# First MoE: layer norm results copied by DMA into float32r tiles, whose transposes use that type

## The chip, the cores and the metric

The kernel runs on one core of one Trainium2 chip. The metric is the device time of one execution in microseconds (us). The engines are named as in the profile: PE is TensorE (PEld its weight loads), DVE VectorE, ACT ScalarE, POOL GpSimd, SP SyncE, which here only issues DMAs.

## What is computed

Attention with a bias from positions (4 batches, 8 heads, 576 positions, head size 64) gives x of 2304 tokens by 512. Two feed-forward layers follow. The first (d_ff 1024) is the one that the change touches, the second has d_ff 2048.

```python
def _moe_ref(x, w_in, w_out, g_ln):
    h = x @ w_in
    h_max = np.max(h, axis=-1, keepdims=True)
    e = np.exp(h - h_max)
    sm = e / (np.sum(e, axis=-1, keepdims=True) + 1e-09)
    solu = h * sm
    mu = np.mean(solu, axis=-1, keepdims=True)
    var = np.mean((solu - mu) ** 2, axis=-1, keepdims=True)
    ln = (solu - mu) / np.sqrt(var + 1e-06) * g_ln
    return (ln @ w_out).astype(np.float32)

def _moe2_ref(x, w_in, w_out):
    h = x @ w_in
    g = np.where(h >= 1, h, np.where(h <= -1, 0.0, (h + 1) ** 2 / 4))
    return (g @ w_out).astype(np.float32)
```

## The kernel before

Most products run in float32r, a float32 of reduced precision: each operand is split into a high part that fits the type and the rest, and a product is three products (high by high, high by rest, rest by high). `g_ln` is multiplied into `w_out` when that is split.

The first MoE works on 18 tiles of 128 tokens, i = 0 to 17. All engines' instructions stand in the order in which the code issues them (the order is written out by hand), and each engine runs its own queue in that order. The functions, by their steps:

- `split_x(i)` splits x of tile i: ACT L528, POOL L529.
- `emit_h(i)` makes h: 24 products of 512 columns on PE (L545) into the PSUM tile `ps_s` (two buffers).
- `emit_post(i)` is softmax, product and layer norm in five steps: DVE L563 (maximum) and ACT L564 (exp); DVE L566, L567, L568 (h times softmax, into the SBUF tile `sc` of 128×1024 float32); DVE L572 and ACT L573 (squares); DVE L575 and POOL L578 (the root); ACT L580 and L581, which write the normalised tile over `sc`. Tiles 0 and 1 use the attention's buffers (`e`), the others the pool `wb`, in which `sc` has three buffers.
- `emit_lt(i)` transposes the tile: eight transposes of 128×128 on PE (L687) into two PSUM tiles `ps_t`, then for each ACT L691 (high part, float32r) and DVE L695 (rest).
- `emit_o(p, half)` multiplies two tiles by `w_out`: 48 products of 256 columns on PE (L706) into `ps_x`, of which there is one buffer; ACT L711 copies it to SBUF and a DMA on ACT's queue (L712) writes it to DRAM.
- `split_w` (`bw`) prepares the second MoE's weights beside all that, by pieces: DVE L302, L305 and L306, ACT L310, DVE L312, POOL L315, ACT L321, POOL L292, with loads and stores on SP's queue.

The loop L752 runs over i = 2 to 17. In iteration i stand h of i, the first step of `emit_post(i)`, the last step of `emit_post(i - 1)` (L580, L581: `drain(bl)`), the transposes of tile i − 2, the middle steps of `emit_post(i)`, the output of a pair (from i = 4 on), and between them three to four steps of `split_w`, four more after every odd i. Behind the loop come the transposes of tiles 16 and 17 and the last four outputs.

DMAs issued by SP and ACT take eight semaphores in turn, so an issue also waits until the transfer that last used its semaphore has landed.

Of the kernel before, what the change touches and what calls it, by code (L numbers as in the profile page):

```python
# [11 lines left out]
F32 = mybir.dt.float32  # L12
F32R = mybir.dt.float32r
# [22 lines left out]
def tile_attention_moe_moe(  # L36
# [11 lines left out]
    nc = tc.nc  # L48
# [3 lines left out]
    def pool(name, side="left", space=None):  # L52
        if space == bass.MemoryType.DRAM:
            return tc.tile_pool(name=name, bufs=1, space=space)
        if space is not None:
            return tc.tile_pool(name=name, bufs=1, space=space, reuse_waits="tile")
        return tc.tile_pool(name=name, bufs=1, side=side, reuse_waits="tile")

    def opened(p):
        es = ExitStack()  # L60
        return es, es.enter_context(p)
# [4 lines left out]
    def flat(ap):  # L66
        return ap.rearrange("p a b -> p (a b)")

    def step(g, n=1):
        for _ in range(n):  # L70
            next(g, None)

    def drain(g):
        for _ in g:
            pass
# [7 lines left out]
    ident = const.tile([128, 128], F32, name="ident")  # L83
# [43 lines left out]
    for _ in range(8):  # L127
# [8 lines left out]
        out=dg[:, 0:32], in_=ident.rearrange("p (a h) -> p h a", a=4), axis=AX.X, op=ALU.max  # L136
# [7 lines left out]
    for _ in range(12):  # L144
# [8 lines left out]
        out=w2b,  # L153
# [227 lines left out]
    def ps_t():  # L381
        return ps.tile([128, 512], F32, tag="t", name="ps_t", bufs=3)
# [38 lines left out]
    def emit_exp(k):  # L421
        u, n = divmod(k, 9)
        i, h0 = divmod(n, 2)
        e, su = e_t[u, i][:, h0, :], su_t[u]
        nc.scalar.activation(  # L425
            out=e, in_=e, func=ACTF.Exp, scale=-1.0, bias=su[:, n:n + 1], accum_out=su[:, 9 + n:10 + n]
        )
# [85 lines left out]
    def split_x(i):  # L513
        if i < 2:
            xh = wq.tile([128, S + 64 * i], F32R, tag=f"kh{i}", name="xh", bufs=2)[:, 0:512]
            xl = wq.tile([128, S + 64 * i], F32R, tag=f"kl{i}", name="xl", bufs=2)[:, 0:512]
            xh = xh.rearrange("p (k t) -> p k t", k=KD)
            xl = xl.rearrange("p (k t) -> p k t", k=KD)
        else:
            xh = wb.tile([128, KD, 128], F32R, tag="xh", name="xh", bufs=2)  # L520
            xl = wb.tile([128, KD, 128], F32R, tag="xl", name="xl", bufs=2)
        t0 = 128 * i
        while t0 < 128 * i + 128:
            b, s0 = divmod(t0, S)
            n = min(S - s0, 128 * i + 128 - t0)
            o = t0 - 128 * i
            src = xb_t[b][:, :, s0:s0 + n]
            nc.scalar.copy(out=xh[:, :, o:o + n], in_=src)  # L528
            nc.gpsimd.tensor_tensor(  # L529
                out=xl[:, :, o:o + n], in0=src, in1=xh[:, :, o:o + n].bitcast(F32), op=ALU.subtract  # L530
            )
            t0 += n
        xs_t[i] = (xh, xl)
# [3 lines left out]
    def emit_h(i):  # L537
        xh, xl = xs_t.pop(i)
        h = ps_s()
        hp_t[i] = h  # L540
        for hf in range(2):
            c0 = hf * 512
            for kk in range(KD):
                for j, (l, r) in enumerate(((xh, wih), (xh, wil), (xl, wih))):
                    nc.tensor.matmul(  # L545
                        h[:, hf, :], lhsT=l[:, kk, :], rhs=r[:, kk, c0:c0 + 512],
                        start=kk == 0 and j == 0, stop=kk == KD - 1 and j == 2,
                    )
            yield

    def emit_post(i):
        h = hp_t.pop(i)
        if i < 2:
            e, sc = [
                flat(wa.tile([128, 2, S], F32, tag="e", name="e", bufs=EB))[:, 0:F1].rearrange("p (a c) -> p a c", a=2)
                for _ in range(2)
            ]
            st = wa.tile([128, 32], F32, tag="su", name="st", bufs=3)
        else:
            e = wb.tile([128, 2, 512], F32, tag="e", name="eb", bufs=1)  # L560
            sc = wb.tile([128, 2, 512], F32, tag="sc", name="scb", bufs=3)
            st = wb.tile([128, 8], F32, tag="st", name="stb", bufs=4)
        nc.vector.tensor_reduce(out=st[:, 0:1], in_=h, axis=AX.XY, op=ALU.max, negate=True)  # L563
        nc.scalar.activation(out=e, in_=h, func=ACTF.Exp, bias=st[:, 0:1], accum_out=st[:, 1:2])  # L564
        yield
        nc.vector.tensor_scalar(out=st[:, 2:3], in0=st[:, 1:2], scalar1=1e-9, scalar2=None, op0=ALU.add)  # L566
        nc.vector.reciprocal(out=st[:, 2:3], in_=st[:, 2:3])  # L567
        nc.vector.tensor_tensor_reduce(  # L568
            out=sc, in0=h, in1=e, scale=st[:, 2:3], scalar=0.0, op0=ALU.mult, op1=ALU.add, accum_out=st[:, 3:4]
        )  # L570
        yield
        nc.vector.tensor_scalar(out=st[:, 4:5], in0=st[:, 3:4], scalar1=-1.0 / F1, scalar2=None, op0=ALU.mult)  # L572
        nc.scalar.activation(out=e, in_=sc, func=ACTF.Square, bias=st[:, 4:5], accum_out=st[:, 5:6])  # L573
        yield
        nc.vector.tensor_scalar(  # L575
            out=st[:, 5:6], in0=st[:, 5:6], scalar1=1.0 / F1, scalar2=1e-6, op0=ALU.mult, op1=ALU.add
        )
        nc.gpsimd.tensor_tensor(out=st[:, 6:7], in0=st[:, 5:6], in1=mhalf, op=ALU.pow)  # L578
        yield
        nc.scalar.activation(out=st[:, 7:8], in_=st[:, 4:5], func=ACTF.Identity, scale=st[:, 6:7])  # L580
        nc.scalar.activation(out=sc, in_=sc, func=ACTF.Identity, scale=st[:, 6:7], bias=st[:, 7:8])  # L581
        ln_t[i] = sc
        yield

    EB, LT, LP = 4, 5, 7
    NK = NU * 9
    load_v(1)
    h_t, ln_t, lt_t, x2_t = {}, {}, {}, {}
# [7 lines left out]
    for k in range(NK + LP + 1):  # L596
        u, n = divmod(k, 9)
        hp, b = divmod(u, B)
        if k == NK:
            emit_T(k - LT)  # L600
            drain(bw)
            drain(emit_h(0))
            bp = emit_post(0)
        for c in order[n] if k < NK else tail.get(n, "TP"):
            if c == "Q":
                emit_qk(k)
                if b == B - 1 and hp + 1 < HP:
                    load_bias(hp + 1, n)
            elif c == "T" and 0 <= k - LT < NK and k != NK:
                emit_T(k - LT)  # L610
            elif c == "E":
                emit_exp(k)
            elif c == "P" and 0 <= k - LP < NK:
                u2, n2 = divmod(k - LP, 9)
                if n2 in (3, 7, 8):
                    emit_pv(u2, n2 // 4)
            elif c in "rRMSN" and u > 0:
                emit_norm(u - 1, c)
            elif c == "B":
                step(bg)  # L620
            elif c == "W" and k >= 6:
                step(bw)
        if k in (NK - 8, NK - 6):
            split_x(0 if k == NK - 8 else 1)
        if k > NK:
            step(bp)
        if k == NK + LT - 1:
            drain(emit_h(1))
            drain(bp)
            es_q.close()  # L630
            es_b, wb = opened(pool("wb"))
            split_x(2)
            bp = emit_post(1)
        elif k == NK + LT + 1:
            split_x(3)
        if n == 5 and 1 <= u < NU - 1:
            load_v(u + 1)
# [35 lines left out]
    def emit_lt(i):  # L673
        ln = flat(ln_t.pop(i))
        p, o = divmod(i, 2)
        if o == 0:
            lt_t[p] = (
                wb.tile([128, K1, 256], F32R, tag="lh", name="lh", bufs=2),
                wb.tile([128, K1, 256], F32R, tag="ll", name="ll", bufs=2),
            )  # L680
        lh, ll = lt_t[p]
        subs = []
        for q in range(2):
            tp = ps_t()
            for j in range(4):
                f = 4 * q + j
                nc.tensor.transpose(tp[:, j * 128:(j + 1) * 128], ln[:, f * 128:(f + 1) * 128], ident)  # L687
            t3 = tp.rearrange("p (f t) -> p f t", f=4)
            dh = lh[:, 4 * q:4 * q + 4, 128 * o:128 * o + 128]
            dl = ll[:, 4 * q:4 * q + 4, 128 * o:128 * o + 128]  # L690
            nc.scalar.copy(out=dh, in_=t3)  # L691
            subs.append((dl, t3, dh))
        yield
        for dl, t3, dh in subs:
            nc.vector.tensor_tensor(out=dl, in0=t3, in1=dh.bitcast(F32), op=ALU.subtract)  # L695
# [56 lines left out]
    for i in range(2, NTT):  # L752
# [6 lines left out]
        if i + 2 < NTT:  # L759
            split_x(i + 2)  # L760
        bp = emit_post(i)
        lt = emit_lt(i - 2)
        step(bp)
# [106 lines left out]
    for s in range(len(seq) + L2):  # L870
        if s < len(seq):
            j, f = seq[s]
# [83 lines left out]
```

## Time and profile before

| what | us |
|---|---|
| median of 3 runs | 977.04 (975.93 to 978.26) |
| profiled execution: its time | 977.47 |
| profiled execution: its span | 975.7 |
| PE busy | 942.9, 97% |
| ACT busy | 545.9, 56% |
| DVE busy | 616.0, 63% |
| POOL busy | 299.9, 31% |

A profile is one execution. Times in its rows count from the start of the span. The time of the execution is 1.8 us longer than the span. A matmul's end is modelled and matmuls overlap in the array, so the distance between two starts tells what one costs, not its duration. ACTq marks what ACT's sequencer does, here the issue of a DMA. In brackets behind a row stands the idle time of the engine before it and what ended that.

### The profile page before, as it was taken

What the parts mean: (1) busy time and instruction counts of PE and PEld (TensorE: products, weight loads), DVE (VectorE), ACT (ScalarE), POOL (GpSimd) and SP (SyncE); (2) the same over time, 40 slices, a digit from 0 to 9 for tenths busy, and PEclk for the clock granted to TensorE, in tenths of its full rate; (3) what the DMA queues carried; (4) which work ended last, traced back from release to release, by engine and by line L of the source; (5) the groups of instructions that cost most, each with busy time, mean ns of one, the idle gap of its engine ahead of it and who ended that gap; (6) DMA issues with size and microseconds to landing.
All of it is one profiled execution on the core that took longest, in us unless ns stands there. A gap on an engine that the chain in (4) does not pass through costs nothing.

```text
span 975.7 us, 15942 instructions
## 1 busy us (share of the span) xinstructions
PE 942.9 (97%) x5972; PEld 780.6 (80%) x5972; DVE 616.0 (63%) x1285; ACT 545.9 (56%) x1132; POOL 299.9 (31%) x255
## 2 busy tenths in 40 slices
PE   7779999999999999999999999899999999999998
PEld 5228888888788878999898988678888888888897
DVE  7988779779789536777776747774434343434343
ACT  5888888889889847666666533343222232222232
POOL 1015555555555213455565523430010011000000
PEclk9999999999999999999999999999999999999999
DMA  4895463563652100244554578501000100100010
GB/s 129 249 291 190 136 217 138 167 211 103 196 190 90 37 22 1 87 131 151 174 172 153 168 290 296 174 1 65 11 12 1 65 22 0 44 16 6 1 44 23
DMA packets 48034, 109.11 MB, mean 112 GB/s; under 512 B 7314, under 2 KB 12434, under 8 KB 47956
## 3 DMA queue, kind: packets, MB, share of 16 engines
q1 hardware_dynamic: 42688, 101.72, 32.0%
q10 hardware_dynamic: 4900, 4.72, 1.4%
q0 software_dynamic: 368, 1.64, 0.5%
q8 instruction: 47, 0.77, 0.3%
q14 instruction: 31, 0.25, 0.1%
HBM read 77.25 MB, written 30.82 MB: 111 GB/s over the span
## 4 chain that ended last, share of the span: by engine, by line
PE 74%; DVE 11%; issue 5%; POOL 4%; ACT 4%; DMA 2%; SPq 0%; POOLq 0%; DVEq 0%; ACTq 0%
PE acc L855 17%; PE h L831 17%; PE ps_s L545 8%; PE ps_s L404 7%; PE ps_x L496 6%; PE ps_x L706 5%; PE ps_t L467 5%; POOL wp L315 2%; DVE r L255 2%; PE ps_x L500 2%; DVE raw L305 2%; PE ps_t L443 1%; PE o L268 1%; POOL wdl L292 1%; DVE wp L302 1%
## 5 line engine op out<-in xcount | busy, mean ns | idle before, releaser
L838 DVE SCALAR_TENSOR_TENSOR ga<-ga 128x512 f32<-128x512 f32 (+1 forms) x80 | 55.7, 696 | 150.9 <-ACT ga L837 150.9
L837 ACT ACTIVATE ga<-h,half_c 128x512 f32<-128x512 f32 (+1 forms) x80 | 51.5, 644 | 128.4 <-PE h L831 128.4
L410 DVE CUSTOM_DVE_ANT_0 e<-ps_s,bt 128x576 f32<-128x576 f32 x144 | 106.7, 752 | 26.3 <-PE ps_s L404 22.2
L831 PE MATMUL h<-x2h,w2h 128*128 128x512 f32 (+1 forms) x320 | 118.5, 370 | 3.9 <-DVE ga L839 3.9
L831 PE MATMUL h<-x2h,w2l 128*128 128x512 f32 (+1 forms) x320 | 117.9, 368 | 0.9 <-DMA w2l<-w_d 0.9
L831 PE MATMUL h<-x2l,w2h 128*128 128x512 f32 (+1 forms) x320 | 117.8, 368 | 0.0
L425 ACT ACTIVATE e<-e,su 128x576 f32<-128x576 f32 x144 | 112.4, 781 | 9.3 <-DVE su L410 8.9
L840 ACT CAST gh<-ga 128x512 fp32r<-128x512 f32 (+1 forms) x80 | 46.2, 578 | 123.4 <-DVE ga L839 123.4
L855 PE MATMUL acc<-w2h,gh 128*128 128x512 f32 x288 | 112.2, 390 | 0.0
L855 PE MATMUL acc<-w2l,gh 128*128 128x512 f32 x288 | 112.2, 390 | 0.0
L855 PE MATMUL acc<-w2h,gl 128*128 128x512 f32 x288 | 112.0, 389 | 0.0
L315 POOL TENSOR_TENSOR wp<-raw,wp 128x256 f32<-128x256 f32 (+1 forms) x64 | 71.7, 1121 | 128.0 <-DVE wp L312 97.4
L404 PE MATMUL ps_s<-kh,sq 128*128 128x288 f32 x320 | 102.1, 336 | 6.4 <-DVE su L410 5.8
L743 POOL TENSOR_TENSOR x2l<-x2f,x2h 128x512 fp32r<-128x512 f32 (+1 forms) x20 | 26.1, 1303 | 246.7 <-ACT x2h L742 246.7
L468 ACT COPY pt<-ps_t 128x512 f32<-128x512 f32 x144 | 83.6, 581 | 23.9 <-PE ps_t L467 23.2
L404 PE MATMUL ps_s<-kl,sq 128*128 128x288 f32 x320 | 89.7, 296 | 0.0
L467 PE MATMUL ps_t<-ident,e 128*128 128x128 f32 x576 | 87.4, 275 | 0.0
L842 DVE TENSOR_TENSOR gl<-ga,gh 128x512 fp32r<-128x512 f32 (+1 forms) x80 | 53.4, 668 | 48.3 <-ACT gh L840 48.1
L706 PE MATMUL ps_x<-lh,woh 128*128 128x256 f32 x256 | 73.4, 287 | 1.3 <-ACT os L711 1.3
L467 PEld LDWEIGHTS ps_t<-ident,e 128*128 128x128 f32 x576 | 69.9, 141 | 5.7 <-ACT pt L468 2.1
L205 POOL TENSOR_TENSOR kl<-stg,kh 128x576 fp32r<-128x576 f32 (+1 forms) x30 | 47.6, 1587 | 86.7 <-DVE kh L202 63.8
L831 PEld LDWEIGHTS h<-x2h,w2h 128*128 128x128 f32 x320 | 60.2, 188 | 17.1 <-DVE ga L839 6.4
(159 smaller groups left out, 2255.0 us busy)
## 6 DMA issues: line engine op xcount, KB each, us to landing
stg<-in_qk_dram SPq DMA_DIRECT2D x30, 640.0 KB, 3.9
raw<-in_w2nd_dram SPq DMA_DIRECT2D x32, 512.0 KB, 4.2
bias_d<-ow SPq DMA_DIRECT2D x36, 295.5 KB, 4.1
w_d<-wdh SPq DMA_DIRECT2D x20, 256.0 KB, 4.2
w_d<-wdl SPq DMA_DIRECT2D x20, 256.0 KB, 3.2
w2h<-w_d SPq DMA_DIRECT2D x10, 512.0 KB, 5.9
w2l<-w_d SPq DMA_DIRECT2D x10, 512.0 KB, 6.2
v<-in_vp_dram SPq DMA_DIRECT2D x15, 320.0 KB, 4.1
```

The source lines that it names most:

```text
L315: nc.gpsimd.tensor_tensor(out=p, in0=t, in1=p, op=ALU.mult)
L404: nc.tensor.matmul(sc[:, hf, 0:HS], lhsT=l, rhs=r, start=j == 0, stop=j == len(parts) - 1)
L410: nc.vector.tensor_tensor_reduce(out=halves(e), in0=sc[:, :, 0:HS], in1=halves(b_t[hp, n]), scale=-1.0 / float(D) ** 0.5, scalar=3.0e38, o ...
L425: nc.scalar.activation(out=e, in_=e, func=ACTF.Exp, scale=-1.0, bias=su[:, n:n + 1], accum_out=su[:, 9 + n:10 + n])
L467: nc.tensor.transpose(tp[:, kt * 128:(kt + 1) * 128], e[:, c0:c0 + 128], ident)
L468: nc.scalar.copy(out=pt[:, 4 * h:4 * h + 4, 128 * o:128 * o + 128], in_=tp.rearrange("p (a b) -> p a b", a=4))
L496: nc.tensor.matmul(x[64 * h:64 * h + 64, o0:o0 + w], lhsT=v[:, kt, 64 * h:64 * h + 64], rhs=r, start=kt == 0, stop=False, skip_group_check ...
L545: nc.tensor.matmul(h[:, hf, :], lhsT=l[:, kk, :], rhs=r[:, kk, c0:c0 + 512], start=kk == 0 and j == 0, stop=kk == KD - 1 and j == 2,)
L706: nc.tensor.matmul(ob[:, a * 256:(a + 1) * 256], lhsT=l, rhs=r[:, f, :], start=f == 0 and j == 0, stop=f == K1 - 1 and j == 2,)
L831: nc.tensor.matmul(hp_, lhsT=l, rhs=r[:, kk, 0:n], start=kk == 0 and q == 0, stop=kk == KD - 1 and q == 2)
L838: nc.vector.scalar_tensor_tensor(out=a, in0=a, scalar=1.0, in1=a, op0=ALU.min, op1=ALU.mult)
L855: nc.tensor.matmul(acc_t[j][q], lhsT=l, rhs=r, start=f == 0 and m == 0, stop=f == K2 - 1 and m == 2)
```

## The change

The normalised tile is no longer transposed from `sc`. A new function `retype(i)` copies it with a DMA on ACT's queue, bit for bit, into a tile `lr` of type float32r (128×1024, 512 KB, two buffers), and the transposes read `lr` and an identity of the same type, `ident_r`, and write PSUM as that type. For tiles 1 to 17 the copy is issued right behind L581, for tile 0 when the pool `wb` is opened. `sc` has two buffers instead of three.

```diff
-            sc = wb.tile([128, 2, 512], F32, tag="sc", name="scb", bufs=3)
+            sc = wb.tile([128, 2, 512], F32, tag="sc", name="scb", bufs=2)
...
         ln_t[i] = sc
+        if i > 0:
+            retype(i)
         yield
+
+
+    def retype(i):
+        lr = wb.tile([128, 2, 512], F32R, tag="lr", name="lr", bufs=2)
+        nc.scalar.dma_start(out=lr.bitcast(F32), in_=ln_t[i])
+        ln_t[i] = lr
...
             es_b, wb = opened(pool("wb"))
+            ident_r = wb.tile([128, 128], F32R, name="ident_r")
+            nc.vector.tensor_copy(ident_r, ident)
+            retype(0)
             split_x(2)
...
-                nc.tensor.transpose(tp[:, j * 128:(j + 1) * 128], ln[:, f * 128:(f + 1) * 128], ident)
+                nc.tensor.transpose(
+                    tp[:, j * 128:(j + 1) * 128].bitcast(F32R), ln[:, f * 128:(f + 1) * 128], ident_r
+                )
```

On PE nothing moves; each block of eight transposes reads other tiles. On ACT one row is added per tile. ACT's queue before, in the middle of the loop, from one copy of the output tile to the next (`scb` is `sc`, `eb` the exponentials, `os` the copied output, `xh` the high part of x, `wp` and `wdh` belong to the weight split):

```order
L711 COPY os<-ps_x 128x512
L712 DMA x_d<-os 128x2x256
L310 ACTIVATE wp_5288<-wp_5288,exp_c 128x512
L321 CAST wdh<-wp_5288 128x512
L528 CAST xh<-xb_1418 128x512
L564 ACTIVATE eb,stb<-ps_s,stb 128x1024
L580 ACTIVATE stb<-stb 128x1
L581 ACTIVATE scb<-scb,stb 128x1024
L691 CAST lh<-ps_t 128x4x128 x2
L310 ACTIVATE wp_5339<-wp_5339,exp_c 128x512
L573 ACTIVATE eb,stb<-scb,stb 128x1024
L321 CAST wdh<-wp_5339 128x512
```

The same stretch of ACT's queue now:

```order
L724 COPY os<-ps_x 128x512
L725 DMA x_d<-os 128x2x256
L310 ACTIVATE wp_5304<-wp_5304,exp_c 128x512
L321 CAST wdh<-wp_5304 128x512
L528 CAST xh<-xb_1418 128x512
L564 ACTIVATE eb,stb<-ps_s,stb 128x1024
L580 ACTIVATE stb<-stb 128x1
L581 ACTIVATE scb<-scb,stb 128x1024
L590 DMA lr<-scb 128x1024
L704 CAST lh<-ps_t 128x4x128 x2
L310 ACTIVATE wp_5357<-wp_5357,exp_c 128x512
L573 ACTIVATE eb,stb<-scb,stb 128x1024
```

The new issue (L590) stands between L581 and the casts of an earlier tile, so everything behind it in the iteration comes after it. At the end, ACT's queue before around the last tile (17):

```order
L310 ACTIVATE wp_6625<-wp_6625,exp_c 128x512
L580 ACTIVATE stb<-stb 128x1
L581 ACTIVATE scb<-scb,stb 128x1024
L691 CAST lh<-ps_t 128x4x128 x2
L321 CAST wdh<-wp_6625 128x512
```

And now:

```order
L310 ACTIVATE wp_6661<-wp_6661,exp_c 128x512
L580 ACTIVATE stb<-stb 128x1
L581 ACTIVATE scb<-scb,stb 128x1024
L590 DMA lr<-scb 128x1024
L704 CAST lh<-ps_t 128x4x128 x2
L321 CAST wdh<-wp_6661 128x512
```

The transposes of tile 17 wait for what that issue moves. Lines behind L561 are shifted by the diff: L687, L691, L695, L706, L711 and L712 of before are L698, L704, L708, L719, L724 and L725 of after.

## Rows read from the trace of the kernel before

**Rows 1.** The page, part 1: busy us (share of the span) xinstructions.

```profile
PE 942.9 (97%) x5972; PEld 780.6 (80%) x5972; DVE 616.0 (63%) x1285; ACT 545.9 (56%) x1132; POOL 299.9 (31%) x255
```

**Rows 2.** Timeline of PE, two iterations: start us, duration us, instruction, count.

```profile
452.81 0.39 PE L545 MATMUL ps_s<-wil,xh 128*128 128x512 f32 x1
453.03 0.39 PE L545 MATMUL ps_s<-wih,xl 128*128 128x512 f32 x1
453.27 1.03 PE L687 MATMUL ps_t<-ident,scb 128*128 128x128 f32 x8
...
454.26 0.28 PE L706 MATMUL ps_x<-ll,woh 128*128 128x256 f32 x1
454.37 0.28 PE L706 MATMUL ps_x<-lh,wol 128*128 128x256 f32 x1
...
465.33 1.04 PE L687 MATMUL ps_t<-ident,scb 128*128 128x128 f32 x8
466.71 0.39 PE L706 MATMUL ps_x<-lh,woh 128*128 128x256 f32 x1 [0.35 <-ACT os L711]
```

**Rows 3.** L145: xcount: duration ns min/median/max, first and last start us.

```profile
L145 PE MATMUL wz<-wt x24: 275/275/377, 6.2 to 8.9; 128*128 128x128 f32 x24
```

**Rows 4.** Timeline of ACT, one iteration.

```profile
452.74 0.58 ACT L711 COPY os<-ps_x 128x512 f32<-128x512 f32 x1
453.35 0.37 ACTq L712 DMA_DIRECT2D x_d<-os  x1
453.76 0.72 ACT L310 ACTIVATE wp<-wp,exp_c 128x512 int32<-128x512 int32 x1 [0.44 <-ACT os L711]
...
459.10 1.25 ACT L581 ACTIVATE scb<-scb,stb 128x1024 f32<-128x1024 f32 x1
460.25 1.05 ACT L691 CAST lh<-ps_t 128x512 fp32r<-128x512 f32 x2
461.19 0.73 ACT L310 ACTIVATE wp<-wp,exp_c 128x512 int32<-128x512 int32 x1
461.81 1.14 ACT L573 ACTIVATE eb<-scb,stb 128x1024 f32<-128x1024 f32 x1
...
466.08 0.58 ACT L711 COPY os<-ps_x 128x512 f32<-128x512 f32 x1
```

**Rows 5.** Timeline of ACT, further copies of the output tile and one extra cast.

```profile
417.23 0.58 ACT L711 COPY os<-ps_x 128x512 f32<-128x512 f32 x1
...
427.73 0.58 ACT L711 COPY os<-ps_x 128x512 f32<-128x512 f32 x1
...
441.08 0.58 ACT L711 COPY os<-ps_x 128x512 f32<-128x512 f32 x1
...
491.03 0.62 ACT L742 CAST x2h<-x2f 128x512 fp32r<-128x512 f32 x1 [0.44 <-ACT os L711]
...
539.87 0.58 ACT L711 COPY os<-ps_x 128x512 f32<-128x512 f32 x1
```

**Rows 6.** Timelines of ACT and PE, normalisation and transposes of tiles 2 and 17.

```profile
377.33 1.25 ACT L581 ACTIVATE scb<-scb,stb 128x1024 f32<-128x1024 f32 x1
...
380.74 1.03 PE L687 MATMUL ps_t<-ident,scb 128*128 128x128 f32 x8
...
550.80 1.24 ACT L581 ACTIVATE scb<-scb,stb 128x1024 f32<-128x1024 f32 x1
...
553.00 1.04 PE L687 MATMUL ps_t<-ident,scb 128*128 128x128 f32 x8
```

**Rows 7.** DMA issues, windows 362:367, 380:560 and 546.5:549: xcount, KB each, median us to landing.

```profile
raw<-in_w2nd_dram SPq DMA_DIRECT2D x1, 512.0 KB, 3.2
...
raw<-in_w2nd_dram SPq DMA_DIRECT2D x22, 512.0 KB, 4.3
...
x_d<-os ACTq DMA_DIRECT2D x1, 256.0 KB, 2.1
```

**Rows 8.** Timeline of PE, start of the second MoE.

```profile
578.26 0.50 PE L831 MATMUL h<-x2h,w2l 128*128 128x512 f32 x1 [0.95 <-DMA w2l<-w_d]
```

## The prediction

> **What bounds the kernel now.** I read the page first: TensorE (PE) is busy for 97% of the span [rows 1], so a cheaper transpose looks like time gained. A busy share is an average, though, so the next view was PE's timeline in the stage that the change touches, the first MoE from 368 to 571 us. One of its iterations is 24 products of L545 (h), eight transposes of L687 and 48 products of L706 (the output). From one block of transposes to the next it takes 465.33 − 453.27 = 12.06 us [rows 2]. In the second iteration shown PE does not go on at once: L706 starts at 466.71, after idle time that the copy of L711 on ScalarE (ACT) ended [rows 2]. The output products have one PSUM tile (`ps_x`, one buffer), and the next ones wait until L711 has copied the last ones out.
>
> So the third view was ACT's timeline [rows 4, 5], read for the starts of L711. From 452.74 to 466.08 they are 13.34 us apart, from 417.23 to 427.73 10.50 us: iterations alternate, since after every second copy four more steps of the weight split are issued. In a long half ACT runs from L581 to L573 without a gap (459.10, 460.25, 461.19, 461.81) [rows 4]; behind L573 come VectorE (DVE) L575, GpSimd L578 and L315, then ACT L321 and L711. A long and a short half make 13.34 + 10.50 = 23.84 us, and two iterations of PE 24.12 us. Two bounds lie 0.28 us apart: PE leads on paper, ACT's chain is right behind it, and in some iterations ahead. That is what the change has to be read against.
>
> **The change part by part.** *Transposes.* 18 tiles of 8 are 144. One costs today: from the first of a block (453.27) to the second L706 (454.26) are 0.99 us, less one L706 of 0.11, so 0.88 for eight, 0.11 each [rows 2]. No float32r transpose stands in the trace. Low end of its price: float32r products of 512 columns start 0.22 apart, of 256 columns 0.11 [rows 2]; 128 columns would be 0.06, so 0.05 saved each, 0.4 per tile, 7 us over 144. High end: a plain float32 product of 128 columns is two records (24 for the 12 calls of L145, 2.7 us), 0.23 each [rows 3], a loss of 0.12 each, 1.0 per tile, 17 us. I take 0.06 to 0.11, since a float32 transpose is already one record and not two. The Trainium skill speaks against a gain here: "TensorE: Matmul & The Clock Gate", section "LDWEIGHTS (loading the stationary operand)", makes a weight load cost its columns over 1.2 GHz, 107 ns for the 128 columns of data that each transpose loads. By that rule the 0.11 stays, which the rows shown fit as well, and the sum would be that of the rival with no gain below.
>
> *The copy's issue.* Each tile gets one DMA on ACT's queue, between L581 and the casts L691. Its price is in the output's DMA: L711 starts at 452.74 and takes 0.58, the issue follows at 453.35 for 0.37, the next instruction starts at 453.76, 0.44 after L711's end. Without an issue ACT's instructions overlap: L691 starts at 460.25, 0.10 before L581 ends [rows 4]. So an issue costs ACT 0.54 us. Queued behind it are L691, L310 and L573, and who waits for those are DVE, GpSimd and, through L711, PE. In a long half all of it lies on the chain.
>
> *The loop.* From L711 at 417.23 to that at 539.87 are 122.64 us [rows 5], five short and five long halves. At 10.50 and 13.34 they would be 119.2. Three hold one more cast (L742, 0.62 long, 0.53 with its overlap) [rows 5], 1.6 together. That leaves 1.9 in which the chain waited; the half from 441.08 [rows 5] to 452.74 [rows 4] alone holds 1.16 of it. Ten issues add 5.4; the 1.9 I give back, since an ACT that comes later no longer waits there. Loop: +3.5. The pair is then 23.84 + 1.08 = 24.92, over PE's 24.12 and far over the 23.3 that PE would need with cheap transposes. PE now waits for the copies, and what the transposes save is more waiting. One long half before the stretch, whose copy ends it at 417.23, adds 0.5.
>
> *The landing.* Transposes now wait for a transfer of 512 KB. A load of that size takes 3.2 us alone and 4.3 in company, a store of half the size 2.1 [rows 7]; no transfer from SBUF to SBUF is in the trace, so 2.1 to 4.3, and I take about 3, 3.4 in company. In the loop there is time: L581 ends at 460.35 [rows 4] and its tile is transposed at 465.33 [rows 2], 5.0 us later. It is short in two places. Tile 2: L581 ends at 378.58, its transposes start at 380.74 [rows 6], 2.2 us. The issue of tile 1 has by then delayed ACT by about 0.4, so the data land near 382.0, and with the saving on this tile PE goes on 1.2 us late (0.3 to 2.3). Tile 17, the last: L581 ends at 552.04, transposes start at 553.00 [rows 6]. With 0.54 of tile 16's issue and 3.4 of transfer the data land near 556.0, 3.0 late, less 0.4 for the cheaper block: 2.6. At the start of the second MoE PE waits for weights that come by DMA (0.95 idle, 578.26) [rows 8]; a later PE finds them landed, so 1.0 goes back. End: +1.6 (0 to 2.5).
>
> *The rest.* Two buffers in place of three for `sc`: a slot comes free when its copy has landed, one iteration before it is written, at no cost; if a transfer took over 10 us, DVE L568 would wait. The DVE copy to `ident_r` comes once, at a quarter of a tile's size, behind a wait that is over. The traffic, 18 copies of 512 KB, I cost at nothing outside the landings.
>
> **Sum.** +1.2 (tile 2) + 0.5 + 3.5 (loop) + 1.6 (end) = +6.8 us. The profiled execution took 977.47, 975.7 of it span, so 984.3; the median of three is 977.04, and from it 983.8. With the ends of the landings and the 1.9 kept or given back: 981 to 986.5.
>
> **The rivals.**
> *PE sets the pace, faster.* If the copies follow PE, not PE the copies, a faster PE pulls the chain along: each iteration's chain begins with a maximum over h, which waits for PE, and ACT, busy for 56% [rows 1], has idle time in which an issue could fall. Tiles 3 to 14 would save 12 × 0.4 = 4.8, the two landings cost 1.2 + 1.6: 977.0 − 2.0 = 975. Against it: the gapless run from L581 to L573, PE's wait for L711, and that with PE at 23.3 per pair even a free issue leaves the chain's 23.84. It decides from a chain under 23.3 per pair.
> *Half absorbed, no change.* More waits go than the 1.9, and the landings are at their low end: 3.5 becomes 1, the sum under 2: 977 to 979.
> *The change does not do what it says.* Transposes stay at 0.11. The loop hides that, as 24.92 is over 24.12; it shows at tile 2 and at the end, 0.4 each: 984.6, inside the forecast's range.
> *float32r is dear at 128 columns, slower still.* At 0.23 a tile costs 1.0 more, and from a rise of 0.4 per tile on PE is the bound again. A pair would be 24.12 + 2.0 = 26.1, ten halves 130.5 instead of 122.6, and with the first tiles, tile 2 and the end some +12: 989.
>
> **How the numbers follow.** ACT's chain sets the end, slower by 4 to 9 us: 0.64, split about evenly between cheap transposes and unchanged ones. Faster rival 0.12, no change 0.11, dear transposes 0.13. A measurement tells this kernel from no change at about 0.2%, 2 us. Faster by more than that 0.13, within it 0.12, slower 0.75. The range leaves out the faster rival and the upper half of the dearest: 976.8 to 988.8.
>
> **What the profile after would show.** Right: ACT's queue holds 18 issues of 0.33 to 0.4 us, and the next ACT instruction starts about 0.44 after L581's end; the copies of the output tile stand some 13.9 and 11.0 apart; PE's wait for them grows from single iterations to most; transposes of tiles 2 and 17 wait for the DMA. Block time of eight transposes: 0.5 or 0.9. Wrong: if the copies keep 13.34 and 10.50, the price of the issue is wrong, and PE's saving shows in full; if PE waits for `lr` in the loop, transfers take over 5 us; if blocks take 1.8 us, the fourth rival holds.

## The result, and the profile after

The changed kernel takes 988.6 us (median of 4 runs, 986.63 to 989.66), the kernel before beside it 976.84 us: 1.1% slower, ratio 1.0111 (95% interval 1.0097 to 1.0126), or 11.8 us by the medians. The forecast was 983.8. The direction came out, and the time lies in the range, near its upper end: the sum of the forecast, +6.8, holds a little over half of what was lost. The profiled execution took 987.95 us, 986.2 of it span, so 10.5 more than before.

The page's line on the engines, which answers to [rows 1], hardly differs: PE's busy time is the same, and ACT's is 1.6 us longer. The 10.5 us are time in which PE is idle.

```profile
PE 942.9 (96%) x5972; PEld 780.1 (79%) x5972; DVE 612.6 (62%) x1286; ACT 547.5 (56%) x1132; POOL 298.5 (30%) x255
```

ACT's timeline, part of one iteration (start us, duration us, instruction, count, idle time before and what ended it), which answers to [rows 4], and the two copies of the output tile that stand where 417.23 and 539.87 stand in [rows 5]:

```profile
419.34 0.58 ACT L724 COPY os<-ps_x 128x512 f32<-128x512 f32 x1
...
444.53 0.58 ACT L724 COPY os<-ps_x 128x512 f32<-128x512 f32 x1
...
447.49 1.25 ACT L581 ACTIVATE scb<-scb,stb 128x1024 f32<-128x1024 f32 x1
448.76 0.48 ACTq L590 DMA_DIRECT2D lr<-scb  x1
449.28 1.08 ACT L704 CAST lh<-ps_t 128x512 fp32r<-128x512 f32 x2 [0.55 <-ACT scb L581]
...
455.16 0.62 ACT L321 CAST wdh<-wp 128x512 fp32r<-128x512 f32 x1 [3.06 <-POOL wp L315]
455.69 0.58 ACT L724 COPY os<-ps_x 128x512 f32<-128x512 f32 x1
...
546.91 0.58 ACT L724 COPY os<-ps_x 128x512 f32<-128x512 f32 x1
```

From L581's start to L704's are 1.79 us (447.49 to 449.28); before, L691 started 1.15 after L581 [rows 4]. An issue costs ACT 0.64 here. Ten halves of the loop take 546.91 − 419.34 = 127.57 us instead of 122.64.

PE's timeline, two iterations, answers to [rows 2]:

```profile
443.12 0.80 PE L698 MATMUL ps_t<-ident_r,lr 128*128 128x128 f32 x8
445.16 0.39 PE L719 MATMUL ps_x<-lh,woh 128*128 128x256 f32 x1 [1.23 <-ACT os L724]
...
456.44 0.79 PE L698 MATMUL ps_t<-ident_r,lr 128*128 128x128 f32 x8
457.07 0.35 PE L719 MATMUL ps_x<-lh,woh 128*128 128x256 f32 x1
457.26 0.28 PE L719 MATMUL ps_x<-ll,woh 128*128 128x256 f32 x1
```

From the list of PE's waits from 360 to 640 us (who waits, for whom; us in total, times, longest) the lines of the first MoE, first of the kernel before, then of the changed one:

```profile
PE ps_x L706 <- ACT os L711: 1.3, 2, 1.0
```

```profile
PE ps_x L719 <- ACT os L724: 8.4, 6, 1.7
PE ps_t L698 <- DMA lr<-scb: 2.4, 2, 2.0
PE ps_t L698 <- DVE stb L575: 1.9, 1, 1.9
```

PE now waits for the output copy in every long half. Of the two waits for `lr` one is that of tile 17; the other, 0.34 us, is the only one in the loop. The last line names DVE, but it is the wait of tile 2's transposes for their DMA: that is issued at 379.27 and takes 2.9 us, as the next rows show, and in e1 and e7, where these transposes read no copy, the wait is absent. ACT's and PE's rows for tiles 2 and 17 answer to [rows 6], with tile 2's issue from the list of DMAs (KB, us to landing) and the wait in the loop between them; the granted clock behind tile 17 (stretch, its length, busy time of PE, PEld, DVE, ACT and POOL, PEclk, DMA share, GB/s) stands below them:

```profile
378.00 1.25 ACT L581 ACTIVATE scb<-scb,stb 128x1024 f32<-128x1024 f32 x1
379.27 0.47 ACTq L590 DMA_DIRECT2D lr<-scb  x1
...
lr<-scb ACTq DMA_DIRECT2D x1, 512.0 KB, 2.9
...
382.29 0.85 PE L698 MATMUL ps_t<-ident_r,lr 128*128 128x128 f32 x8 [1.93 <-DVE stb L575]
...
519.26 0.88 PE L698 MATMUL ps_t<-ident_r,lr 128*128 128x128 f32 x8 [0.34 <-DMA lr<-scb]
...
558.50 1.25 ACT L581 ACTIVATE scb<-scb,stb 128x1024 f32<-128x1024 f32 x1
559.77 0.47 ACTq L590 DMA_DIRECT2D lr<-scb  x1
...
563.69 0.88 PE L698 MATMUL ps_t<-ident_r,lr 128*128 128x128 f32 x8 [2.02 <-DMA lr<-scb]
```

```profile
565.00:569.00 4.00, 4.00 (x23) 4.00 (x23) 2.68 (x5) 2.61 (x5) 2.02 (x2) 0.57 0.80 254
569.00:571.00 2.00, 2.00 (x19) 2.00 (x18) 1.72 (x2) 0.21 (x1) 0.75 (x1) 1.00 0.76 227
```

The copies land after a median of 3.4 us, against the 2.1 to 4.3 taken from [rows 7]:

```profile
lr<-scb ACTq DMA_DIRECT2D x16, 512.0 KB, 3.4
```

The wait that [rows 8] shows is gone: the list of waits of after names none for `w2l`.

**The ledger.** The span is cut at four places that every variant has: the first product of tile 2's h, the third and the thirteenth copy of the output tile (417.23 and 539.87 in [rows 5]), and the first product of the second MoE. What lies ahead of the first cut differs between executions by up to 4.3 us and is not the change. Stage lengths in us, from the starts of these instructions in each profiled execution:

| kernel | to third copy | loop, ten halves | to second MoE | rest |
|---|---|---|---|---|
| before | 54.75 | 122.64 | 31.15 | 404.69 |
| after | 57.08 | 127.57 | 36.34 | 402.90 |
| e1, issues only | 56.18 | 127.44 | 32.32 | 404.42 |
| e2, copies, float32 transposes | 57.20 | 127.43 | 35.12 | 403.81 |
| e3, float32r without copies | 54.38 | 121.91 | 30.95 | 404.47 |
| e4, two output tiles in PSUM | 58.52 | 127.59 | 35.02 | 403.60 |
| e5, before, steps swapped | 52.38 | 121.11 | 33.19 | 404.14 |
| e6, after, steps swapped | 56.21 | 119.71 | 36.77 | 403.05 |
| e7, e6 without copies of tiles 2, 17 | 52.75 | 119.67 | 32.70 | 404.41 |
| e8, issues on SP | 55.89 | 121.95 | 38.60 | 402.19 |
| e9, two issues per tile | 58.46 | 134.07 | 41.22 | 402.23 |
| e10, after without copies of tiles 2, 17 | 55.50 | 128.09 | 31.75 | 404.14 |
| e11, e6 with extra products | 54.74 | 119.77 | 35.54 | 403.27 |

After less before: +2.33, +4.93, +5.19, −1.79, together 10.66; 0.2 less lies ahead of the first cut.

### The profile page after: what moved, and what is told of

The parts are those of the page before. It is cut to its first block, busy times and chain, and to the rows that moved or that the text cites. A ratio compares the mean times of both kernels' runs of the same rounds, so it can differ in the third digit from the quotient of the medians.

```text
span 986.2 us, 16000 instructions
## 1 busy us (share of the span) xinstructions
PE 942.9 (96%) x5972; PEld 780.1 (79%) x5972; DVE 612.6 (62%) x1286; ACT 547.5 (56%) x1132; POOL 298.5 (30%) x255
## 4 chain that ended last, share of the span: by engine, by line
PE 62%; DVE 8%; issue 8%; POOL 8%; ACT 8%; DMA 4%; ACTq 1%; SPq 0%; POOLq 0%; DVEq 0%
PE acc L868 17%; PE h L844 16%; PE ps_s L404 7%; PE ps_x L496 6%; PE ps_t L467 5%; POOL wp L315 4%; DMA bias_d<-ow 2%; PE ps_x L500 2%; POOL wdl L292 2%; PE ps_s L545 2%; PE ps_t L443 1%; DVE raw L305 1%; PE o L268 1%; DVE wp L302 1%; PE ps_t L496 1%
## 5 line engine op out<-in xcount | busy, mean ns | idle before, releaser
L315 POOL TENSOR_TENSOR wp<-raw,wp 128x256 f32<-128x256 f32 (+1 forms) x64 | 71.6, 1119 | 132.6 <-DVE wp L312 103.5
L719 PE MATMUL ps_x<-lh,woh 128*128 128x256 f32 x256 | 74.1, 290 | 8.4 <-ACT os L724 8.4
```

The source lines that it names most:

```text
L315: nc.gpsimd.tensor_tensor(out=p, in0=t, in1=p, op=ALU.mult)
L719: nc.tensor.matmul(ob[:, a * 256:(a + 1) * 256], lhsT=l, rhs=r[:, f, :], start=f == 0 and j == 0, stop=f == K1 - 1 and j == 2,)
```

## The experiments

Each time is a median beside runs of the kernel before on the same chip (977.86 us for e1 to e4, 977.71 for e5 to e8, 977.66 for e9 to e11).

### e1: issues only

```diff
         nc.scalar.dma_start(out=lr.bitcast(F32), in_=ln_t[i])
-        ln_t[i] = lr
```

and the transposes as before.

> The copies are issued as in the changed kernel, but nothing reads them: the transposes read sc in float32 as before. Theory 1 (the issues on ACT's queue lengthen the loop by 4.9 us, and landings and clock cost the rest): PE waits for no copy, the loop's stretch between the copies of the output tile stays near 127.6 us, tile 2 and tile 17 are transposed as early as before but for the issues; 976.8 + 0.6 (first half) + 4.9 (loop) + 0.7 (two issues at the end, less what the second MoE's wait gives back) = 983 (981 to 985). Rival (the landings, not the issues, cost the time): 977 to 978.5, loop near 122.6. Rival (the traffic of the copies slows everything else): 986 or more.

983.92 us, ratio 1.0070 (1.0053 to 1.0088), as theory 1 expected. ACT's copies of the output tile at both ends of the loop:

```profile
416.77 0.58 ACT L721 COPY os<-ps_x 128x512 f32<-128x512 f32 x1
...
544.21 0.58 ACT L721 COPY os<-ps_x 128x512 f32<-128x512 f32 x1
```

The loop loses the same 4.8 us though nobody waits for a copy. Against before the stages give +1.4, +4.8, +1.2 and −0.3: issues alone cost 7.1 of the 10.7.

### e2: copies, but float32 transposes

```diff
-        lr = wb.tile([128, 2, 512], F32R, tag="lr", name="lr", bufs=2)
+        lr = wb.tile([128, 2, 512], F32, tag="lr", name="lr", bufs=2)
```

> The copies are made and waited for as in the changed kernel, but lr is float32 and the transposes are float32. Theory (PE waits for ACT in the loop, so what cheaper transposes save is waiting): a block of eight is 0.2 us longer, the loop's stretch stays near 127.6 us and PE's wait for the copy of the output tile shrinks by 0.2 per iteration; 988.6 to 989.5, or 1 to 2 lower if PE's shorter waits leave the granted clock at full level at 548 us. Rival (transposes are on the path): 18 times 0.2 = 3.5 us more, 992.

987.46 us, ratio 1.0107 (1.0088 to 1.0125). PE's waits in the same stretch:

```profile
PE ps_x L717 <- ACT os L722: 5.0, 6, 1.5
PE ps_t L698 <- DMA lr<-scb: 4.0, 3, 3.5
```

The dearer transposes cost nothing: the same six waits for the output copy shrink from 8.4 to 5.0 us, and the loop stays at 127.4. In this kernel the type brings no time that shows; it only moves PE's waiting. The stage behind the loop is even 1.2 us shorter than in the changed kernel, mainly because the granted clock does not fall in it (its row stands with e11). Against e1 the landings show: +1.0 in the first stage, +2.8 at the end.

### e3: float32r without a copy

```diff
+            ln_t[i] = wb.tile([128, 2, 512], F32R, tag="lr", name="lr", bufs=2)
-        nc.scalar.activation(out=sc, in_=sc, func=ACTF.Identity, scale=st[:, 6:7], bias=st[:, 7:8])
+        nc.scalar.activation(out=ln_t[i], in_=sc, func=ACTF.Identity, scale=st[:, 6:7], bias=st[:, 7:8])
```

for tiles 2 to 17, whose rounded-off part this kernel leaves out.

> No copy for tiles 2 to 17: L581 writes its result straight into a float32r tile, which rounds it, so the low part of the normalised tile is lost; the transposes are float32r. Theory (ACT's chain sets the pace of the loop): the loop's stretch stays at 122 to 122.6 us, and only tile 2 and the two last tiles save 0.2 each: 976 (975 to 977). Rival (PE sets the pace once nothing is added to ACT): 16 tiles at 0.2 = 3.3 us less, 973.5.

976.1 us, ratio 0.9984 (0.9972 to 0.9996), 1.8 less than before. Without copies the loop is 121.91 us, 0.7 less than before; e6 below shows 119.71 where PE does set the pace. The theory holds and the rival, PE as the pace, falls: PE's saving does not come out while the ring of the other engines keeps its length.

### e4: a second PSUM buffer for the output

```diff
-        ob = ps_x() if p < NTT // 2 - 2 or half == 0 else ps_s()[:, 0, :]
+        ob = (ps_x() if half == 0 else ps_t()) if p < NTT // 2 - 2 or half == 0 else ps_s()[:, 0, :]
```

> The changed kernel, but every second output tile of the first MoE goes to a PSUM buffer of ps_t instead of the one ps_x, so PE need not wait for the last copy. Theory (the single ps_x ties PE to ACT's chain): the waits of 1.3 to 1.9 us are gone, a pair of iterations comes to PE's 23.7 to 24 us instead of 25.2, the loop is 6 to 7 us shorter, and the clock does not fall at 548 us: 980 to 982. Rival (ACT's own queue sets the pace, and PE waits elsewhere, at the casts L704, at lr or at the h tile): 987 to 989.

988.76 us, ratio 1.0115 (1.0095 to 1.0135): the rival holds. PE no longer waits for the output copy, and the loop is 127.59 all the same; PE waits for the tile to transpose instead (two of these four waits lie in the loop, two behind it):

```profile
PE ps_t L698 <- DMA lr<-scb: 7.9, 4, 3.0
```

So the one `ps_x` tells PE of the pace, it does not make it. What makes it stands in the timelines of ACT, DVE and POOL of this kernel:

```profile
453.93 1.15 ACT L573 ACTIVATE eb<-scb,stb 128x1024 f32<-128x1024 f32 x1
...
455.20 0.15 DVE L575 TENSOR_SCALAR stb<-stb 128x1 f32<-128x1 f32 x1 [0.95 <-ACT eb L573]
...
455.43 0.93 POOL L578 TENSOR_TENSOR stb<-stb,mhalf 128x1 f32<-128x1 f32 x1 [3.57 <-DVE stb L575]
456.33 1.86 POOL L315 TENSOR_TENSOR wp<-raw,wp 128x512 f32<-128x512 f32 x1
...
458.22 0.62 ACT L321 CAST wdh<-wp 128x512 fp32r<-128x512 f32 x1 [3.06 <-POOL wp L315]
458.75 0.58 ACT L724 COPY os<-ps_t 128x512 f32<-128x512 f32 x1
```

ACT's L321 waits 3.06 us for POOL L315, which is queued behind POOL L578, which waits by DVE L575 for ACT L573. Behind L321 come the copy, in every second iteration one more wait of ACT for L315, the next tile's L564, L580, L581, the new issue, L704 and the next L573; from 453.93 to the next L573 at 468.53 no instruction of ACT waits for PE. That is a closed ring of three queues. PE is not in it, so neither a buffer for PE nor a cheaper transpose shortens it, and an issue of 0.65 us on ACT lengthens it each time.

### e5, e6: one link of the ring taken out

```diff
         drain(lt)
-        step(bp)
         if i >= 4:
             step(bw)
+        step(bp)
```

One step of the weight split (DVE L312, POOL L315) goes ahead of the step with L575 and L578, in the kernel before (e5) and in the changed one (e6).

> The kernel before, with one step of the weight split (DVE L312, POOL L315) queued ahead of the step with DVE L575 and POOL L578 instead of behind it. Theory (the loop's pace is a ring of queues without PE: ACT L573, DVE L575, POOL L578 and L315, ACT L321, then the copy of the output tile): L321 no longer waits for L315 behind L578, the ring is about 1.4 us shorter per iteration, PE sets the pace at 12.06 per iteration, and the loop's stretch of ten falls from 122.6 to 120.6: 974.5 to 975.5. Rival (ACT's own busy time, or something else than that order, sets the pace): stretch unchanged, 976.5 to 978.

> The changed kernel with the same swap of two steps. Theory (ring of queues): the ring has 1.4 us less per iteration and the issue's 0.5 to 0.7 still fits, so PE sets the pace, now with the cheap transposes, 11.87 per iteration: the stretch falls from 127.6 to 118.7 to 119.5, PE's waits for the output copy are gone, and so is the clock's fall at 548 us; the landings at tiles 2 and 17 stay. 977 to 980. Rival (each issue costs its time wherever it stands): the stretch keeps 4.9 us over that of the swapped kernel before, 981 or more.

e5 takes 974.85 us, ratio 0.9972 (0.9961 to 0.9984); e6 979.41, ratio 1.0018 (1.0003 to 1.0032). PE's blocks of transposes, e5 and then e6:

```profile
440.22 1.04 PE L687 MATMUL ps_t<-ident,scb 128*128 128x128 f32 x8
...
452.27 0.93 PE L687 MATMUL ps_t<-ident,scb 128*128 128x128 f32 x7
```

```profile
443.04 0.79 PE L698 MATMUL ps_t<-ident_r,lr 128*128 128x128 f32 x8
...
454.92 0.80 PE L698 MATMUL ps_t<-ident_r,lr 128*128 128x128 f32 x8
```

Now PE sets the pace, 12.05 us per iteration with float32 transposes and 11.88 with float32r, and the loop falls by 1.5 and by 7.9 us (e6's 119.71 is just over the 118.7 to 119.5 expected). The issues, as many and as long as before, cost the loop nothing any more: e6's loop is 1.4 us shorter than e5's. That settles the ring. The rest of the change, landings and clock, stays: e6 is 4.6 us over e5.

### e7 and e10: tiles 2 and 17 not copied

```diff
-        if i > 0:
+        if i > 0 and i not in (2, 17):
             retype(i)
```

Their transposes are the float32 ones of before. e7 has the swap too, e10 not.

> As the changed kernel with the swap, but tiles 2 and 17 are not copied: they are transposed from sc in float32 as before. Theory (the landings of just these two cost 1 us at the first half and 2.8 at the end, the clock's fall there included): 3 to 4.5 us less than the swap alone, 973.5 to 975.5, so at or a little under the swapped kernel before. Rival (another transfer is late instead, at tiles 3 or 16): the waits move to those tiles, 976.5 to 979.

> The changed kernel, but tiles 2 and 17 are not copied: they are transposed from sc in float32 as before; no swap. Theory (landings of these two cost about 1 us and 3 us, the rest is the ring with the issue): loop stretch 127.5 as in the changed kernel, first half and end like the kernel with issues alone: 983 to 985. The fall of the granted clock at 548 us, after a wait of 1.9 us for the output copy, may stay, that at 565 us goes. Rival (landings are at tiles 3 and 16 too): 986 or more.

e7 takes 973.39 us, ratio 0.9957 (0.9943 to 0.9970), the fastest of all; it beats both kernels. Against e6 it is 6.0 less, so landings at two tiles, the issues there and the clock behind them cost more than the 3 to 4.5 expected. It is also 1.5 under e5. These two intervals overlap, but the loops differ by as much, 121.11 and 119.67 us: that is what float32r is worth where PE sets the pace. e10 takes 982.75, ratio 1.0051 (1.0036 to 1.0065): 5.9 us less than the changed kernel, and a little under the 983 to 985 expected; the loop keeps its 128.09. In it the granted clock falls in long halves of the loop; from 420 us on, behind a wait of 1.61 us (PE's timeline, and the stretch with PEclk):

```profile
420.15 0.39 PE L722 MATMUL ps_x<-lh,woh 128*128 128x256 f32 x1 [1.61 <-ACT os L727]
```

```profile
420.00:428.00 8.00, 7.85 (x51) 7.76 (x52) 4.59 (x12) 6.07 (x11) 3.18 (x3) 0.79 0.46 164
```

That makes an output block of 47 steps 7.2 us long instead of 5.7, three times, and the loop is no more than 0.5 longer: PE spends the time that it would have waited.

### e8: issues on SP's queue

```diff
-        nc.scalar.dma_start(out=lr.bitcast(F32), in_=ln_t[i])
+        nc.sync.dma_start(out=lr.bitcast(F32), in_=ln_t[i])
```

> The changed kernel with its copies issued on SP's queue instead of ACT's; no swap. Theory (it is the issue on ACT that lengthens the loop): the stretch falls from 127.6 to 122 to 122.6, landings stay or come a little later, behind loads and stores in SP's queue: 980 to 983. Rival (the copies' traffic lengthens the loop): the stretch stays over 126, 987 or more.

983.75 us, ratio 1.0060 (1.0047 to 1.0072), a little over the 980 to 983 expected. The loop is 121.95, as without copies, with the same bytes moved and with two buffers for `sc`: it was the issue's place, not the traffic and not the third buffer that the change takes away. The end eats the gain: tile 17's copy stands in SP's queue behind a load,

```profile
552.74 1.25 ACT L581 ACTIVATE scb<-scb,stb 128x1024 f32<-128x1024 f32 x1
```

```profile
555.23 0.33 SPq L659 DMA_DIRECT2D raw<-in_w2nd_dram  x1
555.73 0.47 SPq L590 DMA_DIRECT2D lr<-scb  x1
```

1.7 us after L581's end, and PE waits 5.5 us for it:

```profile
560.79 1.00 PE L698 MATMUL ps_t<-ident_r,lr 128*128 128x128 f32 x6 [5.54 <-DMA lr<-scb]
```

The Trainium skill, "DMA: Bandwidth & Descriptors", section "Rules for kernel authors", says that spreading DMAs over issuing engines saves only the issue time of the sequencer. The loop agrees, 5.6 us; the wait at the end is the order of the queue, which that rule does not speak of.

### e9: two issues per tile

```diff
-        nc.scalar.dma_start(out=lr.bitcast(F32), in_=ln_t[i])
+        for c in range(2):
+            nc.scalar.dma_start(out=lr.bitcast(F32)[:, c, :], in_=ln_t[i][:, c, :])
```

> The changed kernel with each copy issued as two halves of 256 KB, so two issues per tile on ACT's queue, the same bytes. Theory (an issue on ACT costs the ring 0.5 us and more): the ten halves of the loop get 10 times 0.5 = 5 us longer, from 127.6 to 132 to 133, first half and end 1 us more: 993 to 996. Rival (the bytes or the wait for landing count, not the issue): stretch 127.6, 988 to 989.

999.48 us, ratio 1.0226 (1.0206 to 1.0245), over the 993 to 996 expected. ACT's timeline:

```profile
450.67 1.14 ACTq L591 DMA_DIRECT2D lr<-scb  x2
451.85 1.08 ACT L705 CAST lh<-ps_t 128x512 fp32r<-128x512 f32 x2 [1.21 <-issue]
```

ACT stands for 1.21 us where one issue made it stand for 0.55: 0.66 for the second, although it moves half as much. Ten of them add 6.5 us to the loop. Half a copy costs ACT as much as a whole one.

### e11: extra products while PE waits

```diff
         subs = []
+        if i in (2, 17):
+            fl = ps_t()
+            for _ in range(7 if i == 2 else 12):
+                nc.tensor.matmul(fl, lhsT=wih[:, 0, 0:128], rhs=wih[:, 0, 0:512], start=True, stop=True)
```

in the kernel of e6.

> The changed kernel with the swap of two steps, and 7 and 12 extra products of 512 columns on PE (1.6 and 2.7 us, results unused) ahead of the transposes of tiles 2 and 17, in the time in which PE only waits for their copies (1.9 and 2.9 us). Theory (the fall of the granted clock to half follows from PE's idle time, and costs 1.5 us each time): the output products behind both waits run at full clock, 5.7 instead of 7.2 us for 47 steps, and the time falls from 979.4 to 976 to 977. Rival (the clock falls for another reason, or the extra products delay the transposes): blocks of 7.2 us stay, 979 to 981.

978.05 us, ratio 1.0004 (0.9994 to 1.0014). The stretch behind tile 2's transposes, in e6 and in e11:

```profile
382.00:390.00 8.00, 7.92 (x56) 7.95 (x57) 6.94 (x13) 5.74 (x10) 2.76 (x3) 0.79 0.17 68
```

```profile
382.00:390.00 8.00, 8.00 (x64) 7.70 (x64) 6.77 (x13) 5.56 (x10) 2.80 (x3) 1.00 0.17 68
```

The clock stays full behind both waits, and the output blocks take 5.7 instead of 7.2 us. So in these two executions the fall goes with PE's idle time. But a wait is not enough for it: in e2 PE waits 3.53 us for tile 17's copy, longer than in any of the waits filled here, and the clock behind it stays full.

```profile
563.21 1.09 PE L698 MATMUL ps_t<-ident,lr 128*128 128x128 f32 x8 [3.53 <-DMA lr<-scb]
...
564.00:568.00 4.00, 4.00 (x36) 4.00 (x35) 2.48 (x5) 2.82 (x5) 1.81 (x2) 1.00 0.79 270
```

What else decides is open. The time lies between the 976 to 977 of the theory and the 979 to 981 of the rival. The gain over e6 is 1.4 us by the medians and 2.6 by the spans of the profiled executions, not the 3 expected for two falls. The record has the granted clock of every run, which suggests why: its mean is 0.9941 over the eleven runs of e6 and 0.9960 over the twelve of e11. One fall, the stretch of 8 us at 0.79 above, takes 8 × 0.21 = 1.7 us of full clock, 0.0017 of such a mean. By this estimate, and if falls elsewhere in the span are alike, e6's executions have on average about one fall more than e11's, not two.

## Why the prediction was right, and where its sizes were not

*What sets the end: right.* ACT's queue, not PE, and an issue on it delays the loop (e1, e8). The main signs held: the issue behind L581, the waits for the output copy in every long half, the waits of tiles 2 and 17. One sign of being wrong came in small: PE waited for `lr` once in the loop, 0.34 us at 519.26, for a transfer that took 4.4 us and not over 5. The first rival, PE as the pace, was rightly put low: e3 shows that even a free copy leaves the ring. PE sets the pace only with the ring cut (e6, e7), and of these two only e7 is faster than before.

*The range: in part luck.* The sum's own bounds were 981 to 986.5, and 988.6 lies above them. It lies in the stated range only because that was drawn up to 988.8 for part of the rival with dear transposes, whose mechanism did not come (see below).

*Why PE waits: right, with one thing left open.* PE's waits are for the copy out of the single `ps_x`, and the prediction names the links behind L573, from DVE L575 by L578 and L315 to L321 and L711. It left open whether the chain needs PE: by its first rival each turn begins with a maximum over h, which waits for PE. e4 shows that it closes without PE. The number was not hurt by that, since the chain was read off ACT's rows.

*The issue's price: too low.* It was taken as 0.54 from the output's DMA [rows 4], whose issue takes 0.37 us. The copy's takes 0.47 to 0.52, and ACT loses 0.64 to 0.66. Ten of these are 6.5; less the 1.9 of waits that the prediction gave back they make 4.6, against 3.5 forecast and 4.93 measured. The term that gives waits back was about right.

*Tile 2 and the first half: 1.7 forecast, 2.33 measured.* The copy landed 2.9 us after L581's end, near the 3 taken, but from the first cut on that L581 stood 0.9 later and not 0.4, behind tile 1's issue (0.9 in e3 too, where tile 1's copy is the last), and the long half lost 0.67 and not 0.5.

*The end: +2.6 forecast, +5.19 measured.* From the thirteenth copy to tile 17's transposes are 16.78 us instead of 13.13 (553.00 − 539.87) [rows 5, 6], 3.65 more. L581 of tile 17 starts 0.66 later, and its result is transposed 3.94 after L581's end (559.75 to 563.69) where 0.96 had passed: a landing of 3.9, not 3.4, and of the 0.4 that a cheaper block was to give back 0.1 came. The other 1.54 is the step that the prediction did not have: behind that wait the granted clock is 0.57 from 565 to 569 us, part of it at 1.2 GHz, part at 2.4. The same fall at 548 us cost nothing, since PE afterwards waits for tile 17's copy anyway; in e2, where it does not occur, tile 17's transposes come 17.09 us after the copy.

*What comes back in the second MoE: 1.0 forecast, 1.79 measured.* The wait of [rows 8] went as said. The rest was not traced; in the lists of PE's waits those for `ga`, which DVE writes in the second MoE, fall from 3.0 to 1.1 us.

*The transposes.* 12.05 less 11.88 us per iteration is 0.17 for eight, 0.02 each: 0.09 instead of 0.11, between the 0.06 and 0.11 of the forecast. The rival of dear transposes, by [rows 3], falls. The Trainium skill ("TensorE: Matmul & The Clock Gate", section "LDWEIGHTS (loading the stationary operand)") allows no gain: 128 columns over 1.2 GHz are an estimate of 107 ns each. This trace has less, and decides. In the kernel as changed either value gives the same time, as the prediction said and e2 shows.

In sum, 6.8 were forecast and 10.7 stand in the ledger. The 3.9 between them are 1.4 from the loop (the issue's price), 0.6 from the start, 1.1 from tile 17's copy and 1.5 from the clock, less 0.8 more given back.

## What to carry to other kernels

A busy share of 97% does not say that an engine sets the pace: look for a ring of waits among the other engines' queues, and test it by giving the busy engine a second buffer, which changes nothing if the ring is elsewhere. A DMA on ACT's queue cost ACT 0.64 to 0.66 us here, for 512 KB as for 256 KB, and in a ring that counts once per turn; take the price from an issue of the same shape or add a margin. A copy between producer and consumer needs slack at every place where it is made, here 2.9 to 3.9 us at tiles 2 and 17. The first and last tiles of the loop have least: leave those on the old path, as e7 does.

## What the runs showed of the hardware

A second issue that moves half the bytes held ACT as long as a whole one, 0.66 us (e9), while the output's DMA, of the same 256 KB, is issued in 0.37 us; why the two differ was not tried. The granted clock fell to the lower level, 1.2 GHz, behind waits of PE of 1.6 to 2.9 us (e10, e6). It did not fall behind every one: tile 2 in the changed kernel waited 1.93 us and tile 17 in e2 3.53 us, and their output blocks ran at full clock. It stayed at the upper level where extra products filled the waits (e11). Each fall in e6 and e10 stretched an output block from 5.7 to 7.2 us, which showed in the time only where PE had nothing to wait for afterwards.
